# Where in the load queue the rows of x, w_r and gate_w stand: behind wq, or behind the gate weights

## Chip, cores, metric

One core of one Trainium2 chip. The metric is the device time of one execution in microseconds (us). In the profile, PE is TensorE's matmuls, PEld its weight loads, DVE is VectorE, ACT ScalarE, POOL GpSimd; SPq is the sequencer of SyncE, which issues the loads.

## The reference, cut to what matters

```
g   = sigmoid((x * gate_w).sum(-1))                       # x: [4, 1, 1024]
q   = x @ wq                                              # wq: [1024, 4096], 8.4 MB
a   = softmax(q k_cache^T * Dh**-0.5) v_cache @ wo        # 4 batches x 32 heads x 8192 keys x 128
r   = x @ w_r
b   = x + sigmoid(r) * (silu(x @ w_gate) * (x @ w_up)) @ w_down   # 1024 x 3584, 7.3 MB each
out = g * a + (1 - g) * b
```

Nearly everything that is read is the two caches: 2 x 268 MB of 576 MB. x, w_r and gate_w are 12 KB together, but nothing can be multiplied before x is there.

## The kernel before

All large loads go through one ring of five slots in SBUF, 32 KB per partition each, and through one queue, SyncE's. A pair of slots is taken in turn; a load waits on the issuing engine until its slots have been read.

```
NS = 5
ring = const.tile([P, NS, RING], BF, name="ring")
def load_pair(src, n, apart=False):
    a = slots(2)                       # the next two slots, modulo 5
    if a + 1 < NS and not apart:       # neighbours: one load for both
        lo = a * RING
        nc.sync.dma_start(out=flat[:, lo:lo + 2 * n], in_=src)
        return [flat[:, lo:lo + n], flat[:, lo + n:lo + 2 * n]]
    ...                                # otherwise one load for each half

wq_at = load_pair(A_wq..., DT // 2 * N)                       # slots 0, 1
x6 = const.tile([NX, D], BF)                                  # six rows, not in the ring
nc.sync.dma_start(out=x6[0:Bn], in_=x2)
nc.sync.dma_start(out=x6[Bn:Bn + 1], in_=B_w_r...)
nc.sync.dma_start(out=x6[Bn + 1:Bn + 2], in_=gate_w...)
...
for t in range(DT):                                           # x, w_r, gate_w turned, all six rows at once
    nc.tensor.transpose(out=xw_ps[:, t, :], in_=x6[:, t:D:DT], identity=identb[0:NX, 0:NX])
...
wq_piece()                  # x @ wq: eight steps, four for each half of wq
q_done()
gates()                     # sigmoids of r and of x . gate_w
gu_piece(B_w_gate, 0)       # loads the gate weights (slots 2, 3), then x @ w_gate: eight steps
# then for each pair d of K slots: k_pair(d): load_pair, VectorE transposes, TensorE products
```

The first pairs of slots are therefore: wq in 0 and 1, the gate weights in 2 and 3, **K pair 0** in 4 and 0 (not neighbours, so two loads, of which the second needs the first half of wq to have been read), **K pair 1** in 1 and 2 (one load, which needs the second half of wq to have been read and, as slot 2 reaches a little into the second half of the gate weights, five of the eight steps of their products done), w_up in 3 and 4, K pair 2 in 0 and 1.

## Time and profile before

| | |
|---|---|
| time | 1345.83 us (1345.19 to 1346.19, 3 runs) |
| read from HBM | 575.7 MB, 428 GB/s over the span |
| busy: TensorE, VectorE, ScalarE | 77%, 46%, 4% |
| DMA engines | 9 tenths or more in 39 of 40 slices |

From the page of before, parts 1, 2 and 3 (busy us and share; one digit for each fortieth of the span; rates in the same slices):

```profile
span 1344.2 us, 7958 instructions
PE 1034.7 (77%) x4536; PEld 226.7 (17%) x2348; DVE 611.8 (46%) x358; ACT 50.6 (4%) x46; POOL 55.4 (4%) x90
...
DMA  9999999999999999999999999999999999999997
GB/s 414 437 430 429 440 428 428 444 433 418 446 430 426 432 435 432 438 429 432 430 435 433 437 435 424 431 430 435 433 425 441 431 426 442 431 424 427 434 424 313
...
HBM read 575.68 MB, written 0.01 MB: 428 GB/s over the span
```

The transfers fill the span from the first slice; no engine that computes comes near it. So time is lost only where the DMA engines run dry. That they do not in the first 120 us is seen in the trace's packets.

SyncE's issues of before from 20 us on (timeline; start, duration, engine, line, operation, destination<-source; of the K loads here the first is the second half of K pair 0, the next K pair 1, then K pairs 2 and 3):

```profile
27.69 0.33 SPq L131 DMA_DIRECT2D ring<-in_A_k_cache_dram  x1
43.94 0.33 SPq L127 DMA_DIRECT2D ring<-in_A_k_cache_dram  x1
56.63 0.33 SPq L127 DMA_DIRECT2D ring<-in_B_w_up_dram  x1
87.96 13.37 SPq L127 DMA_DIRECT2D ring<-in_A_k_cache_dram  x2
```

TensorE's waits of before in the first 62 us, and VectorE's timeline from 49 to 100 us (in the brackets: the idle time before, and what ended it):

```profile
PE small L159 <- DMA x<-in_gate_w_dram: 23.1, 1, 23.1
...
PE o_ps L246 <- DMA ring<-in_B_w_gate_dram: 3.5, 1, 3.5
```

```profile
49.87 8.89 DVE L375 STREAM_TRANSPOSE T<-ring 128x2048 uint32<-128x2048 uint32 x4 [12.99 <-DMA ring<-in_A_k_cache_dram]
59.68 8.89 DVE L375 STREAM_TRANSPOSE T<-ring 128x2048 uint32<-128x2048 uint32 x4 [0.92 <-DMA ring<-in_A_k_cache_dram]
79.04 17.66 DVE L375 STREAM_TRANSPOSE T<-ring 128x2048 uint32<-128x2048 uint32 x8 [10.47 <-DMA ring<-in_A_k_cache_dram]
```

TensorE starts at 23.1 us, when the rows have landed just behind wq, and has to wait once more for the gate weights. K pair 1 is issued at 43.9 us. The DMA engines, one after the other, come to its packets at 57.3 to 59.1 us: it has stood in the queue for 13 us. It lands at 79.0, where VectorE begins on it.

### The profile page before, as it was taken

The page shows a single profiled execution, that of the slowest core. Times are in us where ns is not written, and L with a number is a line of the kernel's source. Part 1 is how long each engine was busy: PE and PEld are TensorE (multiplying, and loading weights), DVE is VectorE, ACT ScalarE, POOL GpSimd, SP SyncE. Part 2 cuts the span into 40 slices and gives each one's busy share as a digit, 9 for nine tenths or more (in the row PEclk, how much of TensorE's full clock was granted, in tenths as well). Part 3 has the DMA queues.
Part 4 walks back from the last instruction along what each step waited for, and adds up shares of the span by engine and source line. Part 5 has one row for each costly group of instructions (what it writes and reads, how often), then busy time and mean ns, then how long its engine had stood idle before and what let it go on. Part 6 is the DMA issues. An engine that isn't in the chain of part 4 may idle for free.

```text
span 1344.2 us, 7958 instructions
## 1 busy us (share of the span) xinstructions
PE 1034.7 (77%) x4536; PEld 226.7 (17%) x2348; DVE 611.8 (46%) x358; ACT 50.6 (4%) x46; POOL 55.4 (4%) x90
## 2 busy tenths in 40 slices
PE   2665877777788787778987779598778678876898
PEld 0111111111111121111211112111111112111221
DVE  1555655544345554336455556146555244556000
ACT  0000100001000010001000010000100010000100
POOL 2000010001000010001000010000100010000100
PEclk9787988988998888899888889898889799889799
DMA  9999999999999999999999999999999999999997
GB/s 414 437 430 429 440 428 428 444 433 418 446 430 426 432 435 432 438 429 432 430 435 433 437 435 424 431 430 435 433 425 441 431 426 442 431 424 427 434 424 313
DMA packets 14174, 576.19 MB, mean 429 GB/s; under 512 B 1582, under 2 KB 1590, under 8 KB 2108
## 3 DMA queue, kind: packets, MB, share of 16 engines
q1 hardware_dynamic: 14132, 575.69, 99.4%
q8 instruction: 27, 0.44, 0.1%
q14 instruction: 7, 0.06, 0.0%
q10 hardware_dynamic: 8, 0.00, 0.0%
HBM read 575.68 MB, written 0.01 MB: 428 GB/s over the span
## 4 chain that ended last, share of the span: by engine, by line
DMA 66%; PE 13%; DVE 11%; issue 9%; ACT 0%; another core or an unknown queue 0%; DVEq 0%; SPq 0%
DMA ring<-in_A_k_cache_dram 53%; PE o_ps L455 11%; DVE T L375 11%; DMA ring<-in_A_v_cache_dram 9%; DMA ring<-in_B_w_gate_dram 3%; PE S_ps L381 2%; DMA ring<-in_A_wo_dram 1%; ACT PB L426 0%; PE small L475 0%; PE acc L246 0%; DVEq L375 0%; ACT OS L467 0%; PE acc L212 0%; ACT res L522 0%
## 5 line engine op out<-in xcount | busy, mean ns | idle before, releaser
L375 DVE STREAM_TRANSPOSE T<-ring 128x2048 uint32<-128x2048 uint32 x256 | 566.6, 2277 | 494.9 <-DMA ring<-in_A_k_cache_dram 483.5
L381 PE MATMUL S_ps<-T,Z 128*128 128x512 bf16 x2048 | 520.2, 409 | 220.8 <-DVE T L375 220.3
L455 PE MATMUL o_ps<-ring,PB 128*32 128x512 bf16 x2048 | 462.2, 389 | 51.8 <-DMA ring<-in_A_v_cache_dram 47.2
L381 PEld LDWEIGHTS <-Z 128*128 128x128 bf16 x1024 | 105.8, 103 | 630.8 <-issue 623.6
L455 PEld LDWEIGHTS <-PB 128*32 128x32 bf16 x1024 | 101.0, 99 | 409.5 <-issue 368.3
L468 DVE SCALAR_TENSOR_TENSOR OS<-o_ps,mE,OS 128x512 f32<-128x512 f32 x8 | 6.0, 750 | 102.4 <-ACT OS L467 102.4
L406 ACT ACTIVATE PTs<-S_ps,negm 128x1024 bf16<-128x1024 f32 x8 | 8.9, 1114 | 965.3 <-DVE negm L403 965.2
L358 POOL TENSOR_TENSOR Z<-qa,mq 128x16 bf16<-128x16 bf16 x32 | 9.1, 286 | 744.7 <-PE S_ps L381 659.6
L428 POOL COPY PB<-PT 32x1024 bf16<-32x1024 bf16 x16 | 30.5, 1904 | 81.4 <-PE o_ps L455 81.0
L426 ACT COPY PB<-PT 32x1024 bf16<-32x1024 bf16 x16 | 30.6, 1911 | 1.5 <-DVE PT L408 1.4
L309 DVE CAST LT<-small 128x64 bf16<-128x64 f32 x2 | 0.5, 225 | 40.8 <-PE small L307 40.8
L159 PE MATMUL small<-identb,x 6*128 6x6 bf16 x8 | 0.6, 197 | 23.1 <-DMA x<-in_gate_w_dram 23.1
L399 POOL PARTITION_ALL_REDUCE gmx<-mex x8 | 3.2, 397 | 341.3 <-DVE mex L396 341.3
L394 DVE TENSOR_REDUCE m<-S_ps 128x1 f32<-128x1024 f32 x8 | 9.8, 1226 | 15.9 <-PE S_ps L381 15.9
L212 PE MATMUL acc<-ring,LT 128*4 128x512 bf16 x64 | 14.9, 378 | 1.9 <-DMA ring<-in_A_wo_dram 1.1
L408 DVE STREAM_TRANSPOSE PT<-PTs 128x1024 bf16<-128x1024 bf16 x8 | 10.0, 1246 | 12.1 <-ACT PTs L406 12.1
L212 PE MATMUL acc<-ring,hT 128*4 128x512 bf16 x56 | 12.2, 379 | 0.0
L467 ACT ACTIVATE OS<-o_ps,mE 128x512 f32<-128x512 f32 x8 | 5.5, 687 | 157.4 <-PE o_ps L455 157.4
L475 PEld LDWEIGHTS small<-selg,OS 128*128 128x128 f32 x64 | 9.0, 208 | 4.1 <-issue 3.9
L475 PE MATMUL small<-selg,OS 128*128 128x16 f32 x64 | 8.7, 269 | 0.0
L246 PE MATMUL o_ps<-ring,xw 128*4 128x512 bf16 x56 | 5.5, 519 | 3.5 <-DMA ring<-in_B_w_gate_dram 3.5
L246 PE MATMUL S_ps<-ring,xw 128*4 128x512 bf16 x64 | 6.4, 590 | 0.3 <-DVE xw L161 0.3
(71 smaller groups left out, 63.9 us busy)
## 6 DMA issues: line engine op xcount, KB each, us to landing
ring<-in_A_k_cache_dram SPq DMA_DIRECT2D x14, 4096.0 KB
ring<-in_A_v_cache_dram SPq DMA_DIRECT2D x14, 4096.0 KB, 31.3
ring<-in_B_w_gate_dram SPq DMA_DIRECT2D x1, 7168.0 KB, 37.9
ring<-in_B_w_up_dram SPq DMA_DIRECT2D x1, 7168.0 KB, 39.2
ring<-in_B_w_down_dram SPq DMA_DIRECT2D x2, 3584.0 KB, 27.8
ring<-in_A_wo_dram SPq DMA_DIRECT2D x6, 1024.0 KB, 21.0
ring<-in_A_v_cache_dram SPq DMA_DIRECT2D x2, 2048.0 KB, 25.7
ring<-in_A_v_cache_dram SPq DMA_DIRECT2D x4, 1024.0 KB, 24.6
```

What stands on the lines that cost most here:

```text
L212: nc.tensor.matmul(out_ap, lhsT=lhsT, rhs=rhs, start=start, stop=True, skip_group_check=True)
L246: nc.tensor.matmul(ps[32 * k:32 * k + Bn, z, :], lhsT=xT[TW * half + t], rhs=cols(w, t, 4 * z + k), start=(half + t == 0), stop=(half == 1 ...
L358: nc.gpsimd.tensor_tensor(out=Z[:, :, QP - 1:QP - 1 + P].rearrange("p e (q c) -> p e q c", c=QP)[:, :, :, 0], in0=qa[:, :, h0:h0 + NQ, b], ...
L375: nc.vector.transpose(out=T[:].rearrange("p j h i e -> p (j h i e)").bitcast(U32), in_=kn[:, c * CJ * Dh:(c + 1) * CJ * Dh].bitcast(U32))
L381: nc.tensor.matmul(sps[:, z, :], lhsT=Z[:, he, s:s + P], rhs=T[:, 16 * z:16 * z + 16, half, :, e], start=(t == 0 and n == 0 and he == 0), ...
L394: nc.vector.tensor_reduce(out=m1[:], in_=sps[:].rearrange("p z n -> p (z n)"), axis=AX.X, op=ALU.max)
L406: nc.scalar.activation(out=PTs[:], in_=sps[:].rearrange("p z n -> p (z n)"), func=ACT.Exp, bias=negm[:, 0:1], scale=scale, accum_out=rs[:, ...
L408: nc.vector.transpose(out=PT[:].rearrange("p j i -> p (j i)"), in_=PTs[:])
L426: nc.scalar.copy(out=Bv[at, :, :, q, :], in_=Pv[at])
L428: nc.gpsimd.tensor_copy(out=Bv[at, :, :, q, :], in_=Pv[at])
L455: nc.tensor.matmul(o_ps[row:row + NM, e, :], lhsT=PB[:, RD * t + c, z, w].rearrange("p e s j -> p (e s j)"), rhs=vn[:, j0 * Dh:(j0 + 4) * ...
L475: nc.tensor.matmul(oT[:, :], lhsT=o_sb[:, q * Dh:(q + 1) * Dh], rhs=selg[:, q].rearrange("p t s -> p (t s)"), start=(q == 0), stop=(q == 3))
```

## The change

The gate weights are loaded right after wq; the three small loads come behind them. The intent is to have the large loads at the head of the queue, without small ones between them.

```
     wq_at = load_pair(A_wq.rearrange("(c t) n -> c (t n)", t=DT), DT // 2 * N)
+    gate_at = load_pair(B_w_gate.rearrange("(c t) f -> c (t f)", t=DT), DT // 2 * F)
     NX = Bn + 2
     x6 = const.tile([NX, D], BF)
     nc.sync.dma_start(out=x6[0:Bn], in_=x2)
...
-    def gu_piece(view, w_i):
-
-        ws = load_pair(view.rearrange("(c t) f -> c (t f)", t=DT), TW * F)
+    def gu_piece(w_i, ws=None):
+
+        if ws is None:
+            ws = load_pair(B_w_up.rearrange("(c t) f -> c (t f)", t=DT), TW * F)
...
-    gu_piece(B_w_gate, 0)
-    side = {1: lambda: (gu_piece(B_w_up, 1), h_done()), GD - 1: wd_piece}
+    gu_piece(0, gate_at)
+    side = {1: lambda: (gu_piece(1), h_done()), GD - 1: wd_piece}
```

## The prediction

> **What bounds the kernel now: the transfers.** The page counts 575.7 MB read at 428 GB/s; its DMA row shows 9 in every slice but the last. By the trace's packets all 16 DMA engines stay occupied from 1.0 us (1.03 after the first issue) through at least 130 us. VectorE is busy 46%, TensorE 77%; the chain of waits is 66% DMA. A compute delay costs time only if it delays an issue until the queue runs dry.
>
> **What the change does.** No bytes, instructions or buffers change. Three small transfers (x, w_r, gate_w; six 2 KB packets of 84 ns) move behind the 7.3 MB of gate weights. The Trainium skill ("DMA: Bandwidth & Descriptors", section "Queues, rings and completion order") says that each DMA engine consumes descriptors in ring order. The trace agrees: wq landed at 22.7 us, gate_w at 23.1, the gate weights at 39.7. So the rows should land at about 40 us, and all that needs x starts 17 us later.
>
> Durations are those of before's timeline:
>
> | event | before, us | after, us (estimate) |
> |---|---|---|
> | x transposes start | 23.15 | 40.0 |
> | wq products | 24.05 to 30.5 | 40.9 to 47.4 |
> | issue, K pair 0 second half (first half of wq read) | 27.7 | 44.5 |
> | gate products start | 39.7 | 53.0 |
> | issue, K pair 1 (5/8 of gate products) | 43.9 | 55 to 57.3 |
> | first K transpose (VectorE in order) | 49.9 | 53.5 |
> | first K matmul | 52.2 | 58 to 59.5 |
> | K pair 1 landed | 79.0 | 79 to 80 |
>
> **On the critical path: nearly nothing,** but only just:
> - The engines reach K pair 0's second half at 47.6 us; 44.5 + 1.03 is 2 us early.
> - They reach K pair 1 between 57.3 us (fastest engine) and 59.1 (slowest). 57.3 + 1.03 = 58.3: the fastest idle up to 1 us, the slowest not at all, and a transfer lands with its slowest engine. If TensorE does the gate products faster (before: five of eight steps took 0.86 us, later ones 0.44), the issue is at 55 and nobody idles.
> - The first K pair's work starts 6 us later; VectorE had 10.5 us to spare before K pair 1 (68.6 to 79.0). w_up is issued at 60.5 instead of 56.6, before its turn at 76.6. From K pair 1 on all is as before.
>
> **Prediction: 1346.1 us**, 1344.8 to 1348.2 in 8 of 10 cases; faster by over 2%: 0.005; within 2%: 0.985; slower by over 2%: 0.01.
>
> **What would show each step.**
> - The x transposes wait for gate_w until 40 us instead of 23.1.
> - TensorE's 3.5 us wait for the gate weights is gone.
> - Issues at 44.5 (second K half) and 55 to 57.3 (K pair 1).
> - GB/s of slices 1 to 3 within 2% of before; K pair 1 landed by 80 us; then before's timeline moved by under 1 us.
>
> **What would make it wrong.** Rows landing over 1 us later than 40 (a slow engine carrying them); gate products slower than 0.86 us per step; more than 1.03 us from issue to first packet. Each would make a hole of 1 to 4 us in the transfers, which nothing later refills, as they never pause. A change over 2% needs a stall of 27 us; I see none.

## The result, and the profile after

1345.54 us (median of 4 runs, 1345.35 to 1346.97) against 1346.01 us of before (4 runs, 1345.19 to 1346.39). A ratio here and below is the mean time of one kernel's fast runs over that of the other's of the same rounds, so not quite the ratio of the medians: 1.0000, 95% interval 0.9982 to 1.0017. The change is not seen in the time.

It is well seen in the trace. The page of after (parts 1 and 2):

```profile
span 1345.3 us, 7957 instructions
...
PE   0675877787798787778977779697778678876897
...
DMA  9999999999999999999999999999999999999997
GB/s 415 426 435 419 439 429 425 441 433 425 435 433 428 444 435 417 443 431 432 431 435 433 429 433 431 433 433 439 429 425 441 427 429 439 423 429 438 429 423 319
```

TensorE does nothing in the first slice (33.6 us) any more, and the DMA row has not changed by a digit. The issues of after from 20 us on, TensorE's waits in the first 62 us, and VectorE's K transposes:

```profile
44.59 0.35 SPq L131 DMA_DIRECT2D ring<-in_A_k_cache_dram  x1
57.26 0.33 SPq L127 DMA_DIRECT2D ring<-in_A_k_cache_dram  x1
60.39 0.33 SPq L127 DMA_DIRECT2D ring<-in_B_w_up_dram  x1
88.96 13.37 SPq L127 DMA_DIRECT2D ring<-in_A_k_cache_dram  x2
```

```profile
PE small L160 <- DMA x<-in_A_x_dram: 40.0, 1, 40.0
PE small L224 <- DVE wrep L222: 1.7, 2, 1.4
```

```profile
53.65 17.82 DVE L377 STREAM_TRANSPOSE T<-ring 128x2048 uint32<-128x2048 uint32 x8
80.04 17.66 DVE L377 STREAM_TRANSPOSE T<-ring 128x2048 uint32<-128x2048 uint32 x8 [8.57 <-DMA ring<-in_A_k_cache_dram]
```

The rows are there at 40.0 us instead of 23.1, the wait for the gate weights is gone, and K pair 1 is issued at 57.3 us instead of 43.9. All of this is what was predicted, to 0.3 us. VectorE still waits 8.6 us for K pair 1, so the late start of the K work is made good before it.

One thing is not as predicted: K pair 1 lands 1.0 us later than before, K pair 2 is issued 1.00 us later, and the span is 1.1 us longer. The chain of waits of after up to 80 us shows the way there; "another core or an unknown queue" is SyncE standing at the semaphore of the gate products, as these run just then:

```profile
1.17 38.81 DMA x<-in_A_x_dram
...
40.94 3.63 PE S_ps L247 x32
...
44.59 0.35 SPq L131
...
45.00 12.23 another core or an unknown queue
...
57.26 22.66 DMA ring<-in_A_k_cache_dram
```

In before, the same load took 34.98 us from issue to landing in the same view, as it stood in the queue first; here it takes 22.66 and hardly queues at all. In the trace's packets, the engines begin on K pair 1 between 58.2 and 59.6 us, the first of them 0.95 us after its issue; the first packets of 15 of the 16 engines last 2.8 to 3.5 us instead of 2.42 (in before, none of K pair 1's is longer than 2.6). So the queue was just about dry in this execution. It was so once before, 10 us earlier: around 48 us, where the engines come to K pair 0's second half, eleven packets lasted 1.4 to 2.2 us instead of 1.21, although that load had been issued at 44.6, some 3 us ahead. Counting the bytes moved against before, the first of these places cost about 0.5 us and the second about 1.0. It was a slow one: its time, 1346.97, is the highest of all that the changed kernel had.

### The profile page after: what moved, and what is told of

Same layout as the page of the kernel before. It is cut to its first block, busy times and chain, and to the rows that moved or that the text cites. A ratio compares the mean times of both kernels' runs of the same rounds, so it can differ in the third digit from the quotient of the medians.

```text
span 1345.3 us, 7957 instructions
## 1 busy us (share of the span) xinstructions
PE 1029.0 (76%) x4536; PEld 225.4 (17%) x2348; DVE 612.2 (46%) x358; ACT 50.6 (4%) x46; POOL 55.4 (4%) x90
## 4 chain that ended last, share of the span: by engine, by line
DMA 67%; PE 11%; DVE 11%; issue 9%; another core or an unknown queue 1%; ACT 0%; DVEq 0%; SPq 0%
DMA ring<-in_A_k_cache_dram 52%; DMA ring<-in_A_v_cache_dram 11%; DVE T L377 11%; PE o_ps L457 9%; DMA x<-in_A_x_dram 3%; PE S_ps L383 2%; DMA ring<-in_A_wo_dram 1%; ACT PB L428 0%; PE S_ps L247 0%; PE acc L247 0%; PE small L477 0%; ACT OS L469 0%; DVEq L377 0%; PE acc L213 0%
## 5 line engine op out<-in xcount | busy, mean ns | idle before, releaser
L430 POOL COPY PB<-PT 32x1024 bf16<-32x1024 bf16 x16 | 30.5, 1904 | 80.3 <-PE o_ps L457 79.9
L410 DVE STREAM_TRANSPOSE PT<-PTs 128x1024 bf16<-128x1024 bf16 x8 | 10.0, 1246 | 12.1 <-ACT PTs L408 12.1
## 6 DMA issues: line engine op xcount, KB each, us to landing
ring<-in_A_v_cache_dram SPq DMA_DIRECT2D x4, 1024.0 KB, 29.8
```

The lines of the kernel that those rows point to most:

```text
L410: nc.vector.transpose(out=PT[:].rearrange("p j i -> p (j i)"), in_=PTs[:])
L430: nc.gpsimd.tensor_copy(out=Bv[at, :, :, q, :], in_=Pv[at])
```

## The experiments

The theory: *the delay of 17 us costs nothing because the queue holds about that much work; what counts is whether K pair 0's second half and K pair 1 are issued before the engines come to them.* Rivals: the hole of 1 us in that trace is chance and the place of the rows does not matter at all; the delay is hidden by slack in the compute, not in the queue; small loads between large ones cost something themselves.

Those with ratios were timed beside before on one chip, in two sets of rounds that share runs of before; its median was 1345.86 us for the first set (9 runs) and 1345.94 for the second (the same 9 and one more). All outputs were correct.

### More traces of the changed kernel: after_again, after_r3, after_r4, before_again

The edit: none.

> The changed kernel unaltered, for precision and a second trace. In the first trace K pair 1 was issued at 57.3 us, its first packets started between 58.2 and 59.6 us, took 2.8 to 3.5 us instead of 2.42, and K pair 1 landed at 80.0 instead of 79.0; from there everything was 1.0 us late. Theory (dry queue): the hole is real. The same long first packets and a landing at 79.9 to 80.2 again, and 0.5 to 1.2 us longer than before over the rounds. Rival (chance of one profile): first packets of 2.42 us or a landing at 79.0 to 79.4, and a ratio of 1.0000 with no sign.

> A third trace of the changed kernel. The first showed K pair 1 issued at 57.3 us and a hole (landed 1.0 us late), the second an issue at 55.2 and none (landed 0.1 us late): in the second TensorE sped up half-way through the wq products. Theory (the margin is as wide as the scatter of TensorE's speed-up): the issue again between 55 and 57.4, and landing and hole follow it: 55.2 goes with 79.2, 57.3 with 80.0. Rival (they have nothing to do with each other): an issue near 55 with a landing at 80, or near 57.3 with 79.

> A fourth trace of the changed kernel, expected as the third.

> A second trace of the kernel before, as a yardstick for what two traces of one kernel differ by. Theory: K pair 1 is issued at 43.9 to 44.5 (held by the landing of the gate weights, so that TensorE's speed matters little), 13 us ahead of the engines; no hole; landed at 78.8 to 79.3.

Measured: after_again 1345.75 us (5 runs), ratio to before 0.9998 (0.9985 to 1.0012): no loss of more than 0.12%. after_r3 took 1345.77, after_r4 1346.19, before_again 1345.29 us, one run each. My expectation for after_again missed: it landed at 79.2 us, where I had expected 79.9 to 80.2.

| trace | wq products, us long | K pair 1 issued | long first packets (over 2.6 us), of 16 | landed |
|---|---|---|---|---|
| after (first) | 6.40 | 57.3 | 15 | 80.0 |
| after_again | 4.99 | 55.2 | 5 | 79.2 |
| after_r4 | 4.99 | 55.1 | 8 | 79.3 |
| after_r3 | 4.94 | 54.5 | 1 | 79.4 |
| before | 6.44 | 43.9 | 0 | 79.0 |
| before_again | 6.56 | 43.4 | 0 | 79.1 |

The TensorE lines of the two kinds of execution, from the timelines of after and of after_again:

```profile
40.94 6.40 PE L247 MATMUL S_ps<-ring,xw 128*4 128x512 bf16 x64 [0.28 <-DVE xw L162]
...
52.98 5.53 PE L247 MATMUL o_ps<-ring,xw 128*4 128x512 bf16 x56
```

```profile
41.05 4.99 PE L247 MATMUL S_ps<-ring,xw 128*4 128x512 bf16 x64 [0.28 <-DVE xw L162]
...
51.47 4.97 PE L247 MATMUL o_ps<-ring,xw 128*4 128x512 bf16 x56
```

A step of these products takes 0.85 us while TensorE is slow and 0.43 to 0.47 us when it is fast. The Trainium skill ("TensorE: Matmul & The Clock Gate", section "Part 1: The HAM clock gate") says that the array starts at half clock and goes to full clock after a window of about 3.4 us of activity, that the window runs freely, and that therefore the moment differs from run to run. The traces agree: their clock records last 3.41 us or a multiple of it, and the first one at full clock starts at 43.8 us in after_again, 2.8 us into the wq products, and at 46.6 in after, 5.7 us into them and 0.7 before their end. That makes 1.4 of the 2.1 us between the two issues of K pair 1; most of the rest comes from the gate products in the same way. (after_r3's issue, earlier than expected, had another cause: its rows were there at 39.5 us, 0.6 before those of after_again.) This scatter of 2 to 3 us in the issue of K pair 1 is as large as the margin that the change leaves. Of the four executions one fell clearly over the edge; it landed 1.0 us late, the other three 0.1 to 0.4 us. after_r3, with the earliest issue and one long packet, did not land first, so differences of 0.3 us at the landing have other causes as well (two traces of before differ by 0.1). The rival "chance of one profile" is right about the time, where no loss is seen; it is wrong about the hole, which goes with the late issue: the one execution issued at 57.3 us has 15 long first packets, the two at 55.1 to 55.2 have 5 and 8, that at 54.5 has one. The same holds at K pair 0's second half: the issue at 44.6 us has the long packets, those at 43.7 to 44.4 in the other three have none. In before the wq products were just as slow and it made no difference, since K pair 1 then waits for the gate weights to land.

### The rows further back: behind_2, behind_4, behind_8

The first half of K pair 0 is cut, and the rows are put behind a quarter (behind_2), a half (behind_4) or the whole (behind_8) of it. Against the changed kernel:

```
     gate_at = load_pair(B_w_gate...)
+    k0_at = slots(2)
+    nx = EIGHTHS * RING // 8
+    nc.sync.dma_start(out=ring[:, k0_at, 0:nx], in_=k0_src[:, 0:nx])
     (the loads of x, w_r and gate_w)
+    if nx < RING:
+        nc.sync.dma_start(out=ring[:, k0_at, nx:RING], in_=k0_src[:, nx:RING])
     ...
     def k_pair(d):      # for d == 0: issues only the second half
```

> x, w_r and gate_w go further back, behind a quarter of the first half of K pair 0, so everything that needs x starts 2.4 us later than in the changed kernel (x transposes at 42.4). Theory: the backlog of the queue is used up, so from here on each us of delay costs one us: K pair 1 issued at 59.7, first packet 60.7, landed at 82.5 (21.8 us after its first packet, as in the changed kernel), total 3.5 us over before, 1349.5. Rival (the place of the rows does not matter, or later slack takes the hole back): 1346 to 1346.5.

> The rows behind one half of the first half of K pair 0: 4.9 us later than in the changed kernel (x transposes at 44.9). Theory: second half of K pair 0 issued at 49.5 (first hole, as the engines are there at 47.7 to 49.2), K pair 1 issued at 62.2, landed at 85.0; total 6.0 us over before, 1352. Rival: 1346 to 1346.5.

> The rows behind the whole first half of K pair 0: 9.8 us later than in the changed kernel (x transposes at 49.8). Theory: second half of K pair 0 issued at 54.4, engines idle from 47.7-49.2 to 55.4; K pair 1 issued at 67.0, landed at 89.8; total 10.8 us over before, 1357. Rival: 1346 to 1346.5; a third (compute, not transfers, pays): a rise, but without idle DMA engines.

Measured, with the engine time without a packet of the load queue between 2.6 and 120 us (a sum over the trace's packets, divided by 16 engines; the first trace of after has about 0.5 by the same count):

| kernel | x there | 2nd half of K pair 0 issued | K pair 1 issued | engines without a packet, us | K pair 1 landed, against before | time, us | over before, us | ratio (95%) |
|---|---|---|---|---|---|---|---|---|
| before | 23.2 | 27.7 | 43.9 | 0.15 | | 1345.86 | | |
| after_again | 40.1 | 44.4 | 55.2 | 0.38 | +0.1 | 1345.75 | -0.1 | 0.9998 (0.9985 to 1.0012) |
| behind_2 | 42.4 | 46.9 | 58.6 | 1.58 | +1.5 | 1347.55 | +1.7 | 1.0010 (0.9998 to 1.0023) |
| behind_4 | 45.1 | 49.6 | 62.4 | 5.14 | +5.4 | 1350.66 | +4.8 | 1.0034 (1.0022 to 1.0047) |
| behind_8 | 49.8 | 54.0 | 64.7 | 7.49 | +7.8 | 1354.76 | +8.9 | 1.0069 (1.0056 to 1.0082) |

From the page of behind_8 (part 2), where the hole falls into the second slice, and from its timelines of SyncE and VectorE:

```profile
DMA  9799999999999999999999999999999999999997
GB/s 418 327 434 431 433 428 424 441 434 424 441 431 420 445 434 419 442 430 425 435 433 432 435 434 431 435 433 434 433 423 443 431 423 438 433 422 443 421 425 321
```

```profile
53.96 0.35 SPq L379 DMA_DIRECT2D ring<-in_A_k_cache_dram  x1
64.69 0.35 SPq L127 DMA_DIRECT2D ring<-in_A_k_cache_dram  x1
```

The first 17 us of delay cost nothing, the next 10 cost 9: the slope goes from zero to nearly one where the queue is used up. The lateness of K pair 1, the idle time of the engines and the loss of the whole kernel agree within 1.5 us in every row, and nothing makes it good in the 1250 us that follow. The idle time leaves out that first packets are slower. Counting the bytes that the load queue has moved takes both in: after 100 MB it is behind before by 1.3 us in after, 2.5, 6.4 and 8.8 us in these three, and after 570 MB still by 1.4, 2.6, 6.4 and 8.8 us (two traces of before differ by 0.2). The rival by which the place of the rows never matters is out. behind_2 alone is not clear of noise in its time. My numbers were too high (3.5, 6.0 and 10.8 us expected over before), because they took over two things from the first trace of after. One is its late issue: K pair 1 was issued 1.1 us before the expected time in behind_2 and 2.3 us in behind_8, where TensorE sped up sooner within the wq products (5.80 and 4.91 us long); in behind_4, where they took 6.50 us, it was at 62.4, with 62.2 expected. The other is the time from the first packet to the landing, 21.8 us there and 21.0 to 21.1 in these three.

### The rows through another queue: behind_8_act

The edit to behind_8: the three small loads are issued as `nc.scalar.dma_start` instead of `nc.sync.dma_start`, so that they do not stand behind the large ones.

> The order of behind_8, but x, w_r and gate_w are issued from ScalarE's queue; the large transfers keep their order and their cuts. Theory: the rows no longer stand behind 17 MB in the same rings, they land before 10 us, TensorE starts with the landing of wq at about 22.7, K pair 1 is issued at 43.9, and all of the cost of behind_8 is gone: 1345.5 to 1346.5. Rival (the cost of behind_8 comes from the different cut or order of the large transfers): 10 us over before, as behind_8.

Measured: 1345.68 us, ratio 1.0000 (0.9986 to 1.0014). All 9 us are back, with the order and the cut of the large loads of behind_8; so these cost nothing, nor do small loads as such. What costs is the place of the rows behind 20 MB in one queue. TensorE in this kernel, from its timeline, and SyncE's issue of K pair 1:

```profile
19.98 0.63 PE L164 MATMUL small<-identb,x 6*128 6x6 bf16 x8 [19.98 <-DMA x<-in_gate_w_dram]
22.96 6.18 PE L251 MATMUL S_ps<-ring,xw 128*4 128x512 bf16 x64 [2.36 <-DMA ring<-in_A_wq_dram]
```

```profile
44.39 0.33 SPq L127 DMA_DIRECT2D ring<-in_A_k_cache_dram  x1
```

A miss: the rows were to be there before 10 us, and came at 20.0. They were issued by 1.9 us; in the packets of ScalarE's queue, rows and completion writes (4-byte packets at the end of a load) go out at 6.7, 9.7, 12.1, 14.6, 17.0 and 19.5 us, a step of 2.4 to 3.0 us, about the 2.42 us of one 64 KB packet of wq. The skill ("DMA: Bandwidth & Descriptors", section "Queues, rings and completion order") says that an engine takes turns between its queues packet by packet. The trace agrees, and shows the price: with 64 KB packets in the other queue, each small step waits for one of them. It was early enough by 2.4 us here.

### K pair 1 in two loads: after_split, behind_8_split

The edit to the changed kernel, and to behind_8: K pair 1 is loaded as two halves with a wait each; the first half needs only wq to have been read, not the gate weights.

```
-        ks = load_pair(kv_view(A_k_cache, d), RING)
+        ks = load_pair(kv_view(A_k_cache, d), RING, apart=d == 1)
```

> The changed kernel, but K pair 1 is loaded as two halves with a wait each: the first half waits only for the second half of wq to be read (about 47.5 us), the second for the gate products (57.3). Theory: work for 10 us stands in the queue again when the engines come to it, first packets of K pair 1 of 2.4 us, landed at 79.0 instead of 80.0, 0.5 to 1.0 us less than the changed kernel, equal to before. Rival (the 1.0 us comes from elsewhere, such as the late work on K pair 0): still landed at 80.0.

> behind_8 with K pair 1 loaded as two halves with a wait each. Theory: two holes made up the cost of behind_8; the second (before K pair 1) goes, as its first half is issued at 57.2, long before the second half of K pair 0 is through at 66; the first (before that half) stays. 7.2 us over before instead of 10.8. Rival (one cause only, the late x): unchanged at 10.8.

Measured: after_split 1345.54 us, ratio 0.9998 (0.9985 to 1.0012); its trace has no long first packet, and engines without a packet for 0.15 us, as in before, although x is just as late (39.7 us). SyncE, from its timeline between 45 and 58 us (the two halves of K pair 1):

```profile
47.05 0.33 SPq L131 DMA_DIRECT2D ring<-in_A_k_cache_dram  x1
```

```profile
56.90 0.33 SPq L131 DMA_DIRECT2D ring<-in_A_k_cache_dram  x1
```

The first half stands in the queue for 10 us again, and the second is not needed before the first is through. So the hole before K pair 1 came from that one wait, not from the late work on K pair 0, which is just as late here. TensorE was as slow in this trace as in the first of after (wq products 6.40 us, gate products 5.55), so it is not the speed-up that closed the hole. VectorE works through from 53 to 89 us without a pause, so its timeline doesn't show when K pair 1 landed; the profile's view of that load does: its second half landed 22.1 us after its issue, at 79.0 us as expected, against 78.9 in before and 79.9 in after by the same count. In the time, nothing was there to be gained: the expected half to one us is not seen, and after_split cannot be told from after_again or from before.

behind_8_split took 1352.90 us, 7.0 over before (7.2 expected), ratio 1.0053 (1.0040 to 1.0065), against 8.9 of behind_8. Engines without a packet: 6.89 us, of which 6.76 before the second half of K pair 0. The second hole is gone and the first is as it was. The two halves of K pair 1 were issued at:

```profile
55.22 0.35 SPq L131 DMA_DIRECT2D ring<-in_A_k_cache_dram  x1
```

```profile
64.32 0.33 SPq L131 DMA_DIRECT2D ring<-in_A_k_cache_dram  x1
```

The split gained 1.9 us of the 3.6 expected, and no run of one kernel overlaps those of the other. The idle time fell by 0.6 us only, but the slow first packets of K pair 1 went too: by the bytes moved after 100 MB, behind_8 is 8.8 us behind before and behind_8_split 7.1. Of this 1.7 us, 1.2 arise at K pair 1; the rest is there before it, as the second half of K pair 0 happened to be issued 0.5 us earlier (53.5 us for 54.0). Two waits made up the cost, as the theory says; with one cause only, the split would have changed nothing.

### The rows first: x_first

The edit to before: the three small loads in front of wq.

> The rows in front of wq, the kernel of before otherwise. Theory: x is there at about 3 us, TensorE starts the wq products when wq lands (22.7 to 23.0 instead of 24.05), but K pair 1 is still held by the landing of the gate weights (issue at 43.9) and the queue never runs dry: the time of before within 0.5 us. Rival (an earlier start of compute is worth its own length): 1.2 us less than before.

Measured: 1346.44 us, 0.5 over before, ratio 1.0006 (0.9992 to 1.0019). The rival's gain of 1.2 us is out. The rows' packets went at 0.9 to 2.0 us; the x transposes ran at 10.1 (they wait for the identity there), and the wq products waited for wq until 23.4. What I had not thought of: wq is now issued at 1.39 us instead of 0.00, everything in the queue comes later by that, and K pair 1 lands at 80.3, 1.3 us later than in before. The loss in the trace is as large as one expects from a queue that never pauses; in the time it is within the noise.

No version here beats before: where the queue does not run dry, there is nothing to win at its head.

## Why the prediction was right

- **What bounds the kernel.** Right. Time followed the idle time of the DMA engines in every run that could be told apart (1.58, 5.14, 6.89 and 7.49 us of idle time: 1.7, 4.8, 7.0 and 8.9 us more; in the last, slow first packets make up the difference).
- **Order of the queue.** Right: rows at 40.0 us (40.0 predicted), wq products at 40.9 (40.9), gate products at 53.0 (53.0), issues at 44.6 and 57.3 us (44.5; 55 to 57.3), w_up at 60.4 (60.5). The other traces gave 54.5 to 55.2 for K pair 1.
- **"The slowest not at all".** This is the step that was off, by 1 us, in the executions with the late issue. I let the fast engines idle until 58.3 us and the slowest go on at 59.1 at once. The trace shows that 15 of 16 engines need 2.8 to 3.5 us for their first packet of K pair 1 instead of 2.42, and the last began at 59.6. What was mis-sized is the lead: I took 1.03 us from issue to first packet for enough. In these traces a load that was issued 2.2 us before the first engine came to it (after_again, after_r4) still had slow first packets, and so had K pair 0's second half in the first trace, about 3 us ahead ("2 us early" by my reckoning). At 2.8 us (K pair 1 in after_r3) there was one, at 3.3 us (K pair 0's second half in after_again and after_r4) none: some 3 us, then, and not 1. K pair 1 landed at 80.04 (79 to 80 predicted) and the timeline of before was moved by 1.00 us ("under 1 us"). In the other three traces the landing was 0.1 to 0.4 us late.
- **GB/s of slices 1 to 3 within 2%.** Slices 1 and 3 differ by 0.2% and 1.2%, slice 2 by 2.5% (426 for 437). In the other traces of after it is 430 to 438.
- **Slack of the late K work.** Right: VectorE still waited 8.6 us for K pair 1 in the first trace.
- **The time.** 1346.1 predicted, 1345.54 measured, no difference to before in two sets of runs. What made it nothing was a margin of some 13 us in the queue ahead of K pair 1, which the change used up but for 0 to 3 us, as TensorE's speed-up falls. Where in 55 to 57.3 us the issue falls the prediction left open, and that is chance here: the one traced execution with the late issue was 1.4 us slower than the other runs of its set. The forecast of the time didn't hang on it: 1.4 us more in every execution would still have been inside the range.

What stays open: why the first packets of a load that was issued late take longer (the very first ones of the kernel, 2.7 to 3.4 us in before, do so too); how often an unprofiled execution falls over the edge, since the times only say that the mean loss is under 0.12%.

## What to carry to other kernels

Where the transfers bound the time, put a number on each load's time in the queue: from its issue to the moment the engines come to it. A delay of compute up to the smallest of these, less about 3 us here, is free, and what goes beyond it is paid nearly in full, so a change that looks free may have used up the margin of the next one. Small operands that everything waits for belong near the head of the queue, or in another queue; ahead of the first large load they only hold that up (by 1.1 to 1.4 us here).

## What the Trainium skill lacked or had wrong

- "DMA: Bandwidth & Descriptors", section "Latency and other measured facts", gives about 600 ns to the first byte of a load that SyncE or ScalarE issues. These traces show 0.95 to 1.03 us from the start of the issue to the first packet (57.26 to 58.21; 0.00 to 1.03); less the 0.33 to 0.39 us of the issue itself it is 0.62 to 0.64, so the page agrees if it counts from the issue's end, which it doesn't say.
- The same page, section "Queues, rings and completion order", has the turns between queues, but not what they cost a small load: 2.4 to 3.0 us for each packet or completion write beside 64 KB packets, 20 us until three loads of 12 KB in all were there.
- No page that I read has the slow first packets of a queue that has just run dry: 2.8 to 3.5 us against 2.42 us for 64 KB.
- No page that I read says how a profile shows the clock before its first change. In before and after the clock column stands at 1.00 while the steps of the wq products take 0.85 us; the traces' clock records only begin at 29.8 and 46.6 us, so the 1.00 before them is no measurement. Nothing here speaks against the page on the clock gate.
